# Attention and two mixtures on one Trainium2 core: decoding of 64-bit weights and the softmax start spread over the engines, with a new order

## The chip, the cores and the metric

The kernel runs on one core of one Trainium2 chip. The metric is the device time of one execution in microseconds (us). Five engines matter: TensorE (PE, with its weight loads shown as PEld), VectorE (DVE), ScalarE (ACT), GpSimd (POOL) and SyncE (SP), which issues nearly all DMAs.

## The reference

```
scores = scale * q @ k^T          # batch 2, 8 heads, 576 positions, 64 wide
                                  # heads 0-3: a local window of 32; heads 4-7: every 32nd position
attn   = exp(masked scores - row max);  attn /= sum(attn) + 1e-9
x      = attn @ v                 # as 1152 tokens x 512
h      = max(x @ w1, x @ w2, x @ w3)          # 512 -> 768, the first MLP
x2     = h @ w_out                            # 768 -> 512
out    = sum over 4 experts e of p[:, e] * (relu(x2 @ we1[e]) @ we2[e])    # 512 -> 1024 -> 512
```

w1, w2, w3 and w_out come as float64. [...] q, k, v, the expert weights and the output are float32.

## The kernel before

**Stages.** The tokens are cut into four blocks i: batch i // 2, and positions 0 to 255 (even i) or 256 to 575 (odd i), so 256 or 320 tokens each. For each block there are four head pairs p (0 and 1 local, 2 and 3 strided). Attention for (i, p) is made of four atoms: `aa` (scores in PSUM on PE, row maximum on DVE, negated and scaled by 0.125 into `anm`, exponentials on ACT with a sum per row), `an` (reciprocal of the sum on DVE, scaling on POOL), `at` (transposes on PE, copied out of PSUM to `pt` by ACT) and `ap` (product with v on PE, then a split of x in two float16 parts by ACT and DVE). The tiny operation that makes `anm` (L270, L272) runs on POOL for odd i and on DVE for even i (`ANM`).

**Weights.** Every matmul of the MLPs uses three float16 products (high x high, high x low, low x high), so each weight is scaled by a power of two and split in a high and a low float16 part. The first MLP's weights come in six groups `fc` (128 columns of w1, w2 and w3: 128 partitions x 1536 numbers, 1536 KB as 64-bit words), w_out in two groups of the same size. Four atoms prepare a group: `lw` (the load; there are two staging buffers, and one is free again when its group is decoded), `wa` (the largest value, which gives the scale), `wd` (the decoding) and `wp` (the split: ACT writes high, DVE writes low, L136 and L137). `lo`, `oa`, `od`, `os` and `op` do the same for w_out.

**Decoding** (`decode64`, L155 to L168) takes four passes over the 1536 numbers, which lie 8 bytes apart: ACT makes the top bits of the low word (L162); ACT takes 2^-112 off the exponent of the high word, in place (L163); DVE picks the sign out of the high word and joins it to the low word (L166, a `scalar_tensor_tensor` with two inputs); DVE shifts the high word by three bits and joins both (L167). If `wa` comes ahead of `wd`, the largest value is a DVE reduction over the raw words (L132); if it comes behind, it is bounded by an ACT sum of absolute values (L129). The decoded group lies in `r`, of which there is one buffer.

**First MLP and experts.** Atom `g` (block, fc) is the first MLP's hidden layer, with ACT, DVE and POOL making the maximum and the split; `go` is the product with w_out. The experts follow, with a form of the matrix product that takes seven block products (L564 to L566), and a second product (mm3, L350 to L352). The preparation of expert 0 (`ew`, `fw`, `xw`, `yw`) and the start of its first product (`m`) are atoms too.

**Order.** `ORDER` lists the atoms; each is traced in that order, and a planner at compile time, with its own costs, orders each engine's instructions from it. An engine runs its instructions in that fixed order, and SP issues its DMAs so as well.

## Time and profile before

| | us |
|---|---|
| three timed runs | 574.89, 577.31, 580.47 (median 577.31) |
| profiled execution: its span, first to last instruction (no other time of it is given) | 576.2 |
| busy in the span: PE, DVE, ACT, POOL | 555.6, 363.6, 265.1, 136.2 |
| mean granted TensorE clock over the span | 0.973 |

A busy time is the union of the engine's instructions; waiting is not in it. A busy PE can still be slow, because the granted clock (1.00 is 2.4 GHz, 0.50 is 1.2 GHz) is another column. A window row gives, for a stretch of the span, each engine's busy time with the count of its instructions, the granted clock and the share of the 16 DMA engines in use.

### The profile page before, as it was taken

Reading aid. Unit: us, or ns where it says so; the run is one execution under the profiler, and the core shown is the slowest. Engines: PE = TensorE matmul, PEld = TensorE weight load, DVE = VectorE, ACT = ScalarE, POOL = GpSimd, SP = SyncE. Lnnn points to the kernel's source line nnn. Section 1 sums busy time; section 2 is a strip of 40 time slices with the busy share of each in tenths; the row PEclk is TensorE's granted clock in tenths of the full one; section 3 lists DMA queues with packets and bytes.
Section 4 is the critical chain, followed back from the end, with each engine's and each line's share of the span. In section 5 each row is a group of like instructions: output and inputs, shape, how many; then the busy total and the mean of one; then the engine's idle time right before and its main releaser. Section 6 shows DMA issues by size and latency. Waiting matters only on the chain.

```text
span 576.2 us, 9839 instructions
## 1 busy us (share of the span) xinstructions
PE 555.6 (96%) x3968; PEld 380.2 (66%) x3968; DVE 363.6 (63%) x674; ACT 265.1 (46%) x561; POOL 136.2 (24%) x118
## 2 busy tenths in 40 slices
PE   6889899999999999899999999999999999999997
PEld 3778788878777778674447875446875446875444
DVE  3887799882781137988755775993765843765111
ACT  4778778681762123657726443605433610433000
POOL 1223374520121101322505211260221200221000
PEclk9588799999999999999999999999999999999999
DMA  8999338100040003004160000350000000000111
GB/s 292 334 359 292 103 136 294 50 2 2 1 147 1 1 1 114 34 1 148 73 219 0 1 2 1 109 178 6 2 1 1 1 0 1 2 1 0 56 55 56
DMA packets 16253, 44.33 MB, mean 77 GB/s; under 512 B 2296, under 2 KB 2552, under 8 KB 15440
## 3 DMA queue, kind: packets, MB, share of 16 engines
q1 hardware_dynamic: 16064, 43.41, 22.6%
q8 instruction: 31, 0.51, 0.4%
q10 hardware_dynamic: 144, 0.30, 0.2%
...
## 4 chain that ended last, share of the span: by engine, by line
PE 82%; DVE 5%; DMA 5%; ACT 4%; issue 2%; POOL 1%; SPq 1%; DVEq 0%; ACTq 0%; POOLq 0%
PE e L352 11%; PE e L350 11%; PE e L351 11%; PE w L564 9%; PE w L566 9%; PE w L565 9%; PE g L350 6%; PE g L351 6%; PE g L352 6%; DMA v<-in_vs_dram 3%; DMA v<-in_vl_dram 2%; PE sps L264 1%; PE tps L310 1%; ACT p L275 1%; PE ops L337 1%
## 5 line engine op out<-in xcount | busy, mean ns | idle before, releaser
L564 PE MATMUL w<-xops,w1ops 128*128 128x256 f16 (+1 forms) x448 | 127.9, 286 | 1.0 <-DVE c L572 1.0
L565 PE MATMUL w<-xops,w1ops 128*128 128x256 f16 (+1 forms) x448 | 128.0, 286 | 0.8 <-DVE xops L473 0.8
L566 PE MATMUL w<-xops,w1ops 128*128 128x256 f16 (+1 forms) x448 | 128.0, 286 | 0.0
L352 PE MATMUL g<-x,w 128*128 128x256 f16 (+1 forms) x288 | 82.4, 289 | 0.8 <-DVE w L137 0.8
L351 PE MATMUL g<-x,w 128*128 128x256 f16 (+1 forms) x288 | 83.1, 290 | 0.0
L350 PE MATMUL g<-x,w 128*128 128x256 f16 (+1 forms) x288 | 81.3, 289 | 1.5 <-DVE t L398 0.6
L586 POOL TENSOR_TENSOR h<-c,h 128x640 f16<-128x640 f32 (+1 forms) x30 | 40.0, 1335 | 173.9 <-ACT h L585 160.5
L699 DVE SCALAR_TENSOR_TENSOR x2acc<-e,coef,x2acc 128x512 f32<-128x512 f32 (+1 forms) x28 | 20.2, 727 | 69.5 <-PE e L352 69.5
L588 ACT ACTIVATE h<-c 128x512 f16<-128x512 f32 (+1 forms) x34 | 23.1, 680 | 86.3 <-DVE c L578 85.7
L350 PE MATMUL e<-st,h 128*128 128x512 f16 (+1 forms) x152 | 55.9, 368 | 0.0
L352 PE MATMUL e<-st,h 128*128 128x512 f16 (+1 forms) x152 | 55.9, 368 | 0.0
L351 PE MATMUL e<-st,h 128*128 128x512 f16 (+1 forms) x152 | 55.9, 368 | 0.0
L352 PE MATMUL e<-w,h 128*128 128x512 f16 x144 | 54.6, 379 | 0.0
L351 PE MATMUL e<-w,h 128*128 128x512 f16 x144 | 54.4, 379 | 0.0
L350 PE MATMUL e<-w,h 128*128 128x512 f16 x144 | 54.0, 379 | 0.0
L565 PEld LDWEIGHTS <-w1ops 128*128 128x128 f16 x448 | 43.8, 98 | 13.2 <-issue 1.4
L566 PEld LDWEIGHTS <-w1ops 128*128 128x128 f16 x448 | 43.8, 98 | 12.4 <-issue 1.4
L564 PEld LDWEIGHTS <-w1ops 128*128 128x128 f16 x448 | 43.8, 98 | 12.0 <-DVE c L577 0.2
L352 PEld LDWEIGHTS <-h 128*128 128x128 f16 x296 | 29.0, 98 | 33.2
L350 PEld LDWEIGHTS <-h 128*128 128x128 f16 x296 | 29.0, 98 | 32.3
L351 PEld LDWEIGHTS <-h 128*128 128x128 f16 x296 | 29.0, 98 | 32.0
L400 POOL TENSOR_TENSOR h<-t,h 128x256 f16<-128x256 f32 (+1 forms) x24 | 22.7, 950 | 85.5 <-ACT h L399 85.5
...
## 6 DMA issues: line engine op xcount, KB each, us to landing
...
qk<-in_qk1l_dram SPq DMA_DIRECT2D x4, 496.0 KB, 11.7
...
```

The lines of the kernel that those rows point to most:

```text
L264: nc.tensor.matmul(s3[:, j, :], qv[:, g, :], t[:, kstep * g : kstep * g + nk], start=False, stop=j == n - 1)
L275: nc.scalar.activation(p3[:, g, :], s3[:, j, :], AF.Exp, bias=ngm[:rows, g : g + 1], scale=0.125, accum_out=sm[:rows, g : g + 1],)
L350: nc.tensor.matmul(psum, lh, rh, start=i == 0, stop=False)
L351: nc.tensor.matmul(psum, lh, rl, start=False, stop=False)
L352: nc.tensor.matmul(psum, ll, rh, start=False, stop=i == n - 1)
L400: nc.gpsimd.tensor_tensor(hh[:, 1, fc, :], t1[:, :n], hh[:, 0, fc, :], ALU.subtract)
L564: nc.tensor.matmul(pt, wh, xh, start=k == 0, stop=False)
L565: nc.tensor.matmul(pt, wh, xl, start=False, stop=False)
L566: nc.tensor.matmul(pt, wl, xh, start=False, stop=k == 1)
L586: nc.gpsimd.tensor_tensor(lo, c[:, b], hi, ALU.subtract)
L588: nc.scalar.activation(hi, c[:, b], AF.Relu)
L699: nc.vector.scalar_tensor_tensor(a, pt[:, z], coef[:, t : t + 1], a, ALU.mult, ALU.add)
```

## The change

- **Decoding.** The sign is no longer joined by a two-input pass: a one-source pass over 16-bit halves writes the sign into the upper half of the low word (`SGN`: DVE for groups 0 to 3 and 7; for 4 to 6 POOL, which multiplies the high word by zero into a bfloat16). The pass for the low bits runs on DVE, POOL or ACT (`LOW`), and so does the exponent's (`REB`). The last joining pass stays on DVE.
- **Scales.** In the new order `wd` stands ahead of `wa` for groups 0, 1, 2 and 4 and both halves of w_out (before: for group 2), so five DVE reductions become ACT sums.
- **Split.** For groups 0 and 3 (`WLO` q) POOL scales in place, ACT copies to high, POOL subtracts to low. The others stay as they were.
- **Softmax start.** The row maximum comes out negated. `SUB` says for each (i, p) how the exponential gets it: `o`, as before, with the factor 0.125 on DVE always; `d`, DVE adds it to the scores, out of PSUM into SBUF, and ACT works from there; `p`, PE adds it in PSUM by a float32 matmul with the identity. `ACC` b (block 3, p 0) takes the row sums by a DVE reduction.
- **Copies of transposes** go to DVE for seven of sixteen (i, p) (`PTC`), and `ARS` swaps which blocks add 1e-9 on POOL.
- **Order.** A new `ORDER`. The load of weight group 0 is now the first on SP, ahead of all q and k, and groups 0 to 2 are decoded earlier relative to the attention.

```diff
-ANM = 'dpdp'
-ARS = 'pppd'
+SUB = 'ddooodpopooooodo'
+ACC = 'ggggggggggggbggg'
+SGN = 'ddddpppd'
+PTC = 'aaddaddaaaaaddda'
+LOW = 'dpdaaadd'
+REB = 'papppaad'
+WLO = 'qddqdd'
+ARS = 'dpdp'
...
 ORDER = """
-    lq02 lq00 lv01 lq01 lw0 lq03 aa00 lv00 lq20 vs0 aa01 aa02 wa0 wd0 an00 at00 an01 lw1 lv21 ap00 at01 lv20
-    an02 aa03 ap01 wp0 at02 an03 ap02 at03 aa20 ap03 lw2 vs2 wa1 an20 at20 lq22 lq21 aa21 wd1 aa22 lq23 an22
...
+    lw0 lq02 lq01 lq00 wd0 aa01 lv01 lq03 lq20 aa02 an02 wa0 aa00 aa03 lv00 vs0 lw1 an00 aa20 wd1 lv21 lq22 an03
+    lq23 aa23 at00 lv20 at02 vs2 an20 aa22 lw2 at20 an01 ap00 at01 lq21 at03 wd2 an22 aa21 wp0 wa1 lq12 an21 lw3
+    ap02 aa12 lq10 at21 lv10 lv11 an23 ap01 ap03 at22 lq13 lq11 ap21 aa11 wa2 an12 wp1 wa3 an11 aa10 lw4 vs1
+    lv31 ap22 an10 at23 at10 lq30 lq31 ap20 wd3 wd4 at12 ap23 aa13 an13 g00 g01 lw5 aa30 lo0 wp2 lq32 g20 wp3
...
+WHI = 'daadaa'
...
-        top = st64[g % 2].bitcast(U16).rearrange("p (n t) -> p n t", t=4)[:, :, 1]
-        nc.scalar.activation(lw, top, AF.Copy, bias=2.0**-14 - 0.5, scale=2.0**-13)
-        nc.scalar.activation(hw, hw, AF.Copy, scale=REBIAS)
+        half = st64[g % 2].bitcast(U16).rearrange("p (n t) -> p n t", t=4)
+        if LOW[g] == "a":
+            nc.scalar.activation(half[:, :, 0], half[:, :, 1], AF.Copy, bias=2.0**-14 - 0.5, scale=2.0**-13)
+        elif LOW[g] == "p":
+            nc.gpsimd.tensor_scalar(half[:, :, 0], half[:, :, 1], 2.0**-13, 2.0**-14 - 0.5, ALU.mult, ALU.add)
+        else:
+            nc.vector.tensor_scalar(half[:, :, 0], half[:, :, 1], 13, None, ALU.logical_shift_right)
+        if SGN[g] == "d":
+            nc.vector.tensor_scalar(half[:, :, 1], half[:, :, 3], 0x8000, None, ALU.bitwise_and)
+        else:
+            nc.gpsimd.tensor_scalar(half[:, :, 1].bitcast(BF16), hw, 0.0, 1.0, ALU.mult, ALU.mult)
+        if REB[g] == "a":
+            nc.scalar.activation(hw, hw, AF.Copy, scale=REBIAS)
+        elif REB[g] == "p":
+            nc.gpsimd.tensor_scalar(hw, hw, REBIAS, 1.0, ALU.mult, ALU.mult)
+        else:
+            nc.vector.tensor_scalar(hw, hw, REBIAS, None, ALU.mult)
         r = rp.tile([128, NP], F32, tag="r", name=nm("r")) if g < NF1 else hw
         gi, ri = hw.bitcast(I32), r.bitcast(I32)
-        nc.vector.scalar_tensor_tensor(lw, gi, -0x80000000, lw, ALU.bitwise_and, ALU.bitwise_or)
         nc.vector.scalar_tensor_tensor(ri, gi, 3, lw, ALU.logical_shift_left, ALU.bitwise_or)
...
-        ngm = sc.tile([128, 6], F32, tag="anm", name=nm("anm"))
         sm = sc.tile([128, 6], F32, tag="asm", name=nm("asm"))
         for g0 in range(0, ng, sb):
             n = min(sb, ng - g0)
...
                 st = ps.tile([128, 512], F32, tag="mm", name=nm("sps"))
             else:
                 st = psa.tile([128, 512], F32, tag="s", name=nm("sps"))
-            s3 = st[:rows, : n * nk].rearrange("p (g k) -> p g k", g=n)
+            flat = st[:rows, : n * nk]
+            s3 = flat.rearrange("p (g k) -> p g k", g=n)
             if loc:
                 mrhs = mkl[:, 0:4, :] if hf == 0 else mkl[:, 1:6, :]
             else:
                 mrhs = mks0[:, :n, :] if hf == 0 else mks1[:, :n, :]
-            nc.tensor.matmul(
-                st[:rows, : n * nk], identb[:, :rows], mrhs.rearrange("p g k -> p (g k)"), start=True, stop=False
-            )
+            nc.tensor.matmul(flat, identb[:, :rows], mrhs.rearrange("p g k -> p (g k)"), start=True, stop=False)
             for j in range(n):
                 g = g0 + j
                 nc.tensor.matmul(
                     s3[:, j, :], qv[:, g, :], t[:, kstep * g : kstep * g + nk], start=False, stop=j == n - 1
                 )
             gs = slice(g0, g0 + n)
-            nc.vector.tensor_reduce(mx[:rows, gs], s3, AX.X, ALU.max)
-            if ANM[i] == "p":
-                nc.gpsimd.tensor_scalar(ngm[:rows, gs], mx[:rows, gs], -0.125, 1.0, ALU.mult, ALU.mult)
+            nc.vector.tensor_reduce(mx[:rows, gs], s3, AX.X, ALU.max, negate=True)
+            top = mx[:rows, gs].unsqueeze(2).to_broadcast([rows, n, nk])
+            pf = p3[:, gs, :]
+            if SUB[4 * i + p] == "o":
+                nc.vector.tensor_scalar(mx[:rows, gs], mx[:rows, gs], 0.125, None, ALU.mult)
+                for j in range(n):
+                    g = slice(g0 + j, g0 + j + 1)
+                    acc_to = dict(accum_out=sm[:rows, g]) if ACC[4 * i + p] == "g" else {}
+                    nc.scalar.activation(pf[:, j], s3[:, j], AF.Exp, bias=mx[:rows, g], scale=0.125, **acc_to)
+                continue
+            if SUB[4 * i + p] == "p":
+                nc.tensor.matmul(s3, ident[:rows, :rows], top, start=False, stop=True, skip_group_check=True)
+                ef = s3
             else:
-                nc.vector.tensor_scalar_mul(ngm[:rows, gs], mx[:rows, gs], -0.125)
-            for j in range(n):
-                g = g0 + j
-                nc.scalar.activation(
-                    p3[:, g, :],
-                    s3[:, j, :],
-                    AF.Exp,
-                    bias=ngm[:rows, g : g + 1],
-                    scale=0.125,
-                    accum_out=sm[:rows, g : g + 1],
-                )
+                nc.vector.tensor_tensor(pf, s3, top, ALU.add)
+                ef = pf
+            if ACC[4 * i + p] == "b":
+                nc.scalar.activation(pf, ef, AF.Exp, scale=0.125)
+            else:
+                for j in range(n):
+                    nc.scalar.activation(
+                        pf[:, j], ef[:, j], AF.Exp, scale=0.125, accum_out=sm[:rows, g0 + j : g0 + j + 1]
+                    )
+        if ACC[4 * i + p] == "b":
+            nc.vector.tensor_reduce(sm[:rows, :ng], p3, AX.X, ALU.add)
...
-            nc.scalar.copy(ptt[:nk, : n * rows], tps[:nk, : n * rows])
+            if PTC[4 * i + p] == "a":
+                nc.scalar.copy(ptt[:nk, : n * rows], tps[:nk, : n * rows])
+            else:
+                nc.vector.tensor_copy(ptt[:nk, : n * rows], tps[:nk, : n * rows])
             pts_of[i, p].append((c0, n, ptt))
 
     def att_p(i, p):
...
 
     def split_w(fc):
         hi, lo = [ws[fc][j].rearrange("p w k f -> p (w k f)") for j in range(2)]
-        split(hi, lo, groups[fc][2], wsc[fc])
+        r = groups[fc][2]
+        if WLO[fc] == "d":
+            if WHI[fc] == "a":
+                nc.scalar.activation(hi, r, AF.Copy, scale=wsc[fc])
+            else:
+                (nc.gpsimd if WHI[fc] == "p" else nc.vector).tensor_scalar(hi, r, wsc[fc], 1.0, ALU.mult, ALU.mult)
+            nc.vector.scalar_tensor_tensor(lo, r, wsc[fc], hi, ALU.mult, ALU.subtract)
+        else:
+            nc.gpsimd.tensor_scalar(r, r, wsc[fc], 1.0, ALU.mult, ALU.mult)
+            nc.scalar.copy(hi, r)
+            nc.gpsimd.tensor_tensor(lo, r, hi, ALU.subtract)
```

## Rows read from the trace of the kernel before

**Rows 1.** Windows: stretch, width, busy by engine, clock, DMA share, GB/s.
```profile
10.00:30.00 20.00, 14.78 (x83) 11.78 (x84) 17.00 (x34) 16.21 (x50) 5.55 (x10) 0.56 1.02 336
30.00:70.00 40.00, 35.06 (x331) 30.09 (x329) 31.55 (x61) 31.79 (x96) 15.07 (x22) 0.84 0.85 260
70.00:130.00 60.00, 57.99 (x624) 49.83 (x621) 54.17 (x95) 45.31 (x118) 27.24 (x25) 1.00 0.33 116
130.00:260.00 130.00, 127.69 (x995) 96.88 (x994) 73.39 (x154) 55.61 (x105) 21.71 (x19) 1.00 0.10 33
```

**Rows 2.** Windows of 10 us inside the stretch 30 to 70, same columns.
```profile
40.00:50.00 10.00, 8.07 (x78) 6.68 (x78) 9.30 (x13) 9.15 (x30) 4.40 (x7) 0.83 1.02 319
...
60.00:70.00 10.00, 9.84 (x77) 8.68 (x78) 7.05 (x14) 8.15 (x21) 3.41 (x6) 0.66 0.33 89
```

**Rows 3.** Timeline, 37.5 to 42: start, us, instruction, [idle before <-releaser].
```profile
37.58 1.65 ACT L162 ACTIVATE st<-st 128x1536 int32<-128x1536 uint16 x1
...
41.93 0.36 PE L259 MATMUL sps<-mk,identb 128*128 128x480 bf16 x1 [1.98 <-ACT p L275]
```

**Rows 4.** Timeline, 55 to 60.5, same columns.
```profile
55.04 1.75 DVE L132 TENSOR_REDUCE vm<-v 108x1 f32<-108x1536 f32 x1 [1.83 <-DMA v<-in_vs_dram]
...
57.17 1.75 DVE L166 SCALAR_TENSOR_TENSOR st<-st 128x1536 int32<-128x1536 int32 x1
...
57.34 1.63 POOL L270 TENSOR_SCALAR anm<-amx 120x3 f32<-120x3 f32 x1 [2.00 <-DVE amx L268]
...
60.16 0.43 PE L259 MATMUL sps<-mk,identb 128*120 128x324 bf16 x1 [2.89 <-ACT p L275]
```

**Rows 5.** DVE groups by form, 0 to 180: busy us, mean ns, idle.
```profile
L166 DVE SCALAR_TENSOR_TENSOR st<-st 128x1536 int32<-128x1536 int32 x8 | 15.6, 1953 | 2.2 <-ACT st L163 2.2
L137 DVE SCALAR_TENSOR_TENSOR w<-r,s,w 128x1536 f16<-128x1536 f32 x6 | 11.1, 1843 | 0.3 <-ACT w L136 0.3
...
L132 DVE TENSOR_REDUCE mx<-st 128x1 bf16<-128x1536 f32 x5 | 8.7, 1743 | 0.5 <-DMA st<-in_w_dram 0.4
...
L397 DVE TENSOR_TENSOR t<-t,g 128x320 f32<-128x320 f32 x7 | 3.4, 481 | 7.1 <-PE g L352 5.6 <-ACT t L396 1.5
...
L105 DVE RECIPROCAL s<-sinv 128x1 f32<-128x1 f32 x6 | 0.9, 147 | 0.0
...
L182 DVE CAST identb<-ident 128x128 bf16<-128x128 f32 x1 | 0.2, 226 | 0.2 <-POOL ident masks.py:199 0.2
```

**Rows 6.** ACT groups by form, 0 to 180, same columns.
```profile
L162 ACT ACTIVATE st<-st 128x1536 int32<-128x1536 uint16 x8 | 13.2, 1651 | 1.8 <-DMA st<-in_wo_dram 1.7
...
L312 ACT COPY pt<-tps 108x360 f32<-108x360 f32 x8 | 3.7, 466 | 4.2 <-PE ops L337 4.2
...
L129 ACT ACTIVATE w<-r 128x1536 f16<-128x1536 f32 x1 | 1.5, 1484 | 0.3 <-DVE r L167 0.3
```

**Rows 7.** POOL groups by form, whole span, same columns.
```profile
L523 POOL TENSOR_TENSOR st<-st,st 128x1024 f32<-128x1024 f32 x3 | 7.9, 2640 | 29.9 <-DMA st<-in_we_dram 26.7 <-issue 3.2
L270 POOL TENSOR_SCALAR anm<-amx 120x3 f32<-120x3 f32 x8 | 8.8, 1102 | 9.6 <-DVE amx L268 9.5
...
L298 POOL TENSOR_TENSOR p<-p,ar 128x480 f32<-128x480 f32 x4 | 4.0, 991 | 4.2 <-DVE ar L297 4.2
```

**Rows 8.** PE group by form, 0 to 180, same columns.
```profile
L264 PE MATMUL sps<-qk 128*120 128x108 f32 x48 | 7.0, 283 | 0.0
```

**Rows 9.** Timeline at 87 us: a DVE instruction beside a long POOL one.
```profile
86.28 2.22 POOL L298 TENSOR_TENSOR p<-p,ar 128x480 f32<-128x480 f32 x2 [2.48 <-DVE ar L297]
...
87.32 2.79 DVE L166 SCALAR_TENSOR_TENSOR st<-st 128x1536 int32<-128x1536 int32 x1 [0.85 <-ACT st L163]
```

**Rows 10.** Timeline of the start: first DVE, PE and ACT work of the attention.
```profile
5.90 1.00 PE L264 MATMUL sps<-qk 128*128 128x64 f32 x8
...
8.08 1.21 DVE L132 TENSOR_REDUCE vm<-v 64x1 f32<-64x1024 f32 x1 [6.52 <-DMA v<-in_vs_dram]
...
10.06 0.34 ACT L275 ACTIVATE p<-sps,anm 128x96 f32<-128x96 f32 x1 [7.40 <-DVE anm L272]
```

More of the change, by code (lines that the diff above doesn't have):

```diff
@@ L37 @@
 ORDER = """
-    lq02 lq00 lv01 lq01 lw0 lq03 aa00 lv00 lq20 vs0 aa01 aa02 wa0 wd0 an00 at00 an01 lw1 lv21 ap00 at01 lv20
-    an02 aa03 ap01 wp0 at02 an03 ap02 at03 aa20 ap03 lw2 vs2 wa1 an20 at20 lq22 lq21 aa21 wd1 aa22 lq23 an22
-    lq10 ap20 aa23 an21 at21 ap21 wp1 at22 g00 lv11 an23 g01 lq12 lw3 lv10 wa3 at23 ap22 lq11 lv30 wd2 ap23
-    wa2 lq32 wd3 wp2 g20 g21 wp3 g03 aa11 an11 aa10 an10 aa12 vs1 lq13 lq30 at10 g23 at11 ap11 an12 lv31 lw4
-    ap10 at12 g02 wa4 wd4 wp4 lw5 lq31 wa5 lq33 wd5 aa13 aa30 wp5 an30 ap12 an13 aa33 g04 at13 ap13 aa31 vs3
-    at30 g24 ap30 lo0 an31 an33 aa32 g22 at31 at33 lo1 ap31 ap33 an32 at32 g25 oa0 od0 ap32 oa1 od1 os fo op4
-    op0 ew op1 g05 ew g10 fw ew op5 ew op2 op3 fw ew go20 go00 g11 ew ew go03 ew go23 go22 go21 ew go01 go02
-    ew xw g14 g12 g30 ew ew xw g32 ew g13 ew xw g15 ew ew g31 xw xw xw g33 g34 g35 ew xw cl fw xw xw go30 go10
-    go32 go13 go12 go31 m go33 fw m go11 m yw m fw yw yw yw fw yw yw fw fw yw yw yw
+    lw0 lq02 lq01 lq00 wd0 aa01 lv01 lq03 lq20 aa02 an02 wa0 aa00 aa03 lv00 vs0 lw1 an00 aa20 wd1 lv21 lq22 an03
+    lq23 aa23 at00 lv20 at02 vs2 an20 aa22 lw2 at20 an01 ap00 at01 lq21 at03 wd2 an22 aa21 wp0 wa1 lq12 an21 lw3
+    ap02 aa12 lq10 at21 lv10 lv11 an23 ap01 ap03 at22 lq13 lq11 ap21 aa11 wa2 an12 wp1 wa3 an11 aa10 lw4 vs1
+    lv31 ap22 an10 at23 at10 lq30 lq31 ap20 wd3 wd4 at12 ap23 aa13 an13 g00 g01 lw5 aa30 lo0 wp2 lq32 g20 wp3
+    g21 g03 ap10 lv30 at11 aa31 wa5 ap12 ap11 wd5 at13 vs3 g23 lq33 aa32 an30 g22 wa4 lo1 od1 g02 an32 at30 ap13
+    aa33 wp4 g10 ap30 oa1 wp5 od0 oa0 g04 g25 at32 an33 g14 ap32 os at33 an31 at31 ap31 ap33 g05 g24 fo ew op0
+    op1 ew fw op4 op2 ew op5 op3 go00 go20 ew go23 go21 go22 ew fw go02 g30 g12 fw go01 ew go03 g31 ew xw xw g33
+    ew ew g34 g11 ew fw ew g15 xw g32 xw ew xw g13 ew xw xw go10 g35 ew go30 ew go12 go33 cl go32 fw ew xw ew
+    go31 m m go11 go13 m yw fw yw fw yw xw fw yw yw yw yw m yw yw
 """
+WHI = 'daadaa'
 TINY = 2.0**-100
```

## The prediction

> **What bounds the kernel.** I read the windows first. PE works at the full clock and almost without a break from 130 us on, so time is to be had only where PE is idle or slow. I count a stretch's loss as idle time plus busy time x (1 - clock) [rows 1]. From 10 to 30 it is 5.2 + 14.8 x 0.44 = 11.7 us; from 30 to 70, 4.9 + 35.1 x 0.16 = 10.5; from 70 to 130, 2.0; from 130 to 260, 2.3. Together 26.5 us. In the same stretches DVE and ACT are busy for about 80% of the time up to 70, and DVE for 90% from 70 to 130. The DMA engines are full from 10 to 30 (share 1.02), and 0.85 from 30 to 70.
>
> Second, the timeline at PE's two long breaks between 30 and 70. PE stands 1.98 us before 41.93, for exponentials that ACT reaches only behind the two decoding passes of weight group 2, of which the first begins at 37.58 [rows 3]. It stands 2.89 us before 60.16: DVE's reduction of v comes first (55.04, 1.75 us), then POOL's tiny `anm` takes 1.63 us, because DVE's sign pass (57.17, 1.75 us) began just ahead of it and POOL ends only when that one does [rows 4]. After each break the clock falls: 0.83 in 40 to 50 and 0.66 in 60 to 70, against 1.00 in dense stretches [rows 1, 2]. So the first break costs 1.9 idle + 8.07 x 0.17 = 3.3 us, the second 2.9 + 9.84 x 0.34 = 6.2 us: 9.5 of the 10.5.
>
> **The change, engine by engine.** These sums are work in the stretch up to 130 us, not path.
>
> *DVE loses* eight sign passes of 1.953, five reductions of 1.743 and two low splits of 1.843 [rows 5]: 15.6 + 8.7 + 3.7 = 28.0 us. *It gains* ten one-source passes over 1536 numbers (five signs, four low, one exponent). No row shows one. The CAST, one source from SBUF to SBUF, takes 226 ns for 128, and a one-column operation 147 ns, so 0.62 ns a number: 1.10 us at the fast end; the reduction over the same 1536 takes 1.74 at the slow end [rows 5]. I take 1.10, as the CAST is nearest in kind: 11.0 us (17.4 at the other end). Twelve copies of transposes of 365 numbers on average, priced by the read of PSUM with 320 in 481 ns: 0.53 each, 6.3 us. Five subtractions `d`, of 379: 0.54 each, 2.7. One sum `b`, 0.65. Four more `anm` and four more 1e-9, at 0.15: 1.2. Sum 21.9, net **-6.1 us** (up to +0.3).
>
> The page "VectorE: DVE Perf Modes" of the Trainium skill (Mode 2×_2P) states that a one-source operation with both ends in SBUF passes two elements a cycle; by it the ten passes would be an estimated 9.5 us, and DVE's net -7.6. No row here has such a pass of this length.
>
> *ACT loses* five low passes and five exponent passes (same shape, both counted at 1.651) and twelve copies of 0.466, and gains five sums of 1.484 [rows 6]: -16.5 - 5.6 + 7.4 = **-14.7 us**. The split of groups 0 and 3 leaves ACT one pass, as before. Where `d` is used, ACT's exponential has the same count and reads SBUF: counted as nothing; it hides among the others.
>
> *POOL loses* the twelve `anm` (1.10 each, nearly all of it waiting) and gains ten one-source passes and two subtractions of 1536. Its own row of 480 in 991 ns gives 3.2 us for 1536; ACT's 1.65 for this shape is the fast end; I take 3.2, as it is POOL's own. The subtraction: 2.640 for 1024, so 4.0 [rows 7]. So +32 + 7.9 - 13.2 = **+27 us** (fast end, with 3.2 for the subtraction: +9.7). POOL has room: 15.1 of 40 us busy from 30 to 70 and 27.2 of 60 behind it [rows 1].
>
> **What of it lies on the path.**
>
> *Start (10 to 30).* The load of group 0, 1536 KB, goes ahead of all q and k on SP's queue; at 336 GB/s [rows 1] the first scores come 4.7 us later than at 5.90. But DVE was held by a reduction of v until 9.3, and ACT's first exponential came at 10.06 [rows 10]. Scores at 10.6, 1.0 of matmuls, a maximum and a subtraction of 0.5 each: about 12.2, some 2 us late. Against that, group 0 is decoded while the engines wait, and its passes no longer come between exponentials: 1 back. I take **+1.0**, bounds +4.7 (all of the delay) and -3 (its decoding, two ACT passes of 1.65, all won). The queue behind holds the same first eight transfers, so nothing later than 16 us is moved by this.
>
> *`p` matmuls.* Three of 344 columns in float32, 7.0 us / 48 for 108 columns [rows 8]: 0.47 each, 1.4, half in idle time: **+0.7** (0 to 1.4).
>
> *30 to 70.* Group 2's low and exponent passes leave ACT (DVE and POOL take them), and no `anm` is left on POOL, so both causes of the two breaks go, and with them the falls of the clock. What is late next: DVE's reduction of v still stands ahead of a maximum, and DVE has a subtraction more. I leave 1.0 for it: **-8.5**, bounds 0 and -10.5.
>
> *70 to 130.* Here too `anm` waits behind DVE passes, but PE has other work: half of 2.0, **-1.0** (0 to -2.0). *130 to 260.* The order of the experts' preparation changes; I see no sign for it: **0** (-2.3 to +2.3).
>
> Sum +1.0 + 0.7 - 8.5 - 1.0 = -7.8 us on the profiled execution's span of 576.2: 568.4. The page gives no other time of that execution; its span is 1.1 below the median of the runs, 577.31, which I add: **569.5 us**.
>
> **The rivals.**
>
> *A, no change.* The stretch's pace is the DMA's (share 1.02 from 10 to 30 [rows 1]) and the bytes are the same; a break that is taken out comes back at the next transfer, like the 1.83 us for which DVE waits for v at 55.04 [rows 4]. Against it: neither break of PE was a wait for a transfer that the change leaves as it is, save that one. Then only start, `p` and the 1.0 behind 70 count: 576.2 + 0.7 + 1.1 = 578. The one-source passes running at the slow end, so that the sign's new form saves little (DVE net +0.3), ends here too.
>
> *B, slower: POOL and DVE hold each other.* Rows 4 show POOL waiting for a two-input DVE pass, and a DVE pass that takes 1.75 alone takes 2.79 behind POOL's long multiplications [rows 4, 9]. Twelve long POOL passes, 40 us, meet a DVE busy 80 to 90%. If DVE waits for half of them, it loses 20 and keeps 6.1 of relief: +13.9, half of which PE feels: +7; with start and `p`, 576.2 + 8.7 + 1.1 = **586**. It decides once DVE waits for more than about 6 us in all. For it: DVE is the fuller engine. Against it: in rows 4 it is POOL that waits, and that costs only the decoding's own delay.
>
> The page "SBUF — State Buffer" of the Trainium skill (Who interferes with whom) has the rule: one pair of ports, held for a whole instruction, by POOL or by a DVE instruction with two SBUF inputs, and also by a one-source one in a two-port mode. By that last part the ten new DVE passes would hold POOL as well, which no row here shows.
>
> *C, a larger gain.* With ACT 14.7 us lighter and group 0 ready early, PE is dense from 30 on and 4 us of the start's loss go too: -10.5 - 2.0 - 2.3 - 4 + 0.7 = -18: 559.
>
> **The numbers.** A difference of 1% (5.8 us) is about what this kernel's runs can tell from none: faster is under 571.5, slower above 583.1. Forecast 0.48, spread over 563 to 576 by its bounds, two thirds of it under 571.5 (0.33). C 0.20. A 0.15. B 0.17. Faster 0.33 + 0.20 = 0.53; same 0.15 + 0.15 = 0.30; slower 0.17. The range reaches from C's centre to the near edge of B: 558 to 582, leaving out most of B and the far half of C's lower side, some 0.2.
>
> **What would show it.** Right: no break of PE over 1.5 us between 30 and 70, a clock above 0.95 there, ACT's busy time down by 10 to 15 us up to 130, and one-source DVE passes near 1.1 us. Start right: first exponential at 11 to 12.5 us. Wrong: DVE passes of 3 us and more beside long POOL ones (B); breaks as long as before with transfers as their releasers (A); a loss behind 130 of over 4 us, which no term here holds.

## The result and the profile after

The change is slower by 0.9%: 581.25 us against 576.32 us, medians of 12 runs each, ratio 1.0092 [1.0066, 1.0117]. The forecast was 569.5. The profiled execution took 581.21 us with a span of 579.1, so some 2 us lie outside a span (1.8 in later executions of the kernel before). By that the profiled execution of before (span 576.2) was some 1.7 us over its median: the spans differ by 2.9 us, the medians by 4.9.

Windows of the changed kernel, same columns as [rows 1]:

```profile
10.00:30.00 20.00, 17.20 (x82) 14.34 (x82) 16.63 (x37) 9.58 (x45) 10.70 (x7) 1.00 1.03 326
30.00:70.00 40.00, 34.12 (x323) 28.19 (x323) 36.33 (x69) 28.96 (x86) 14.95 (x16) 0.96 0.68 240
70.00:130.00 60.00, 57.86 (x581) 48.70 (x581) 47.30 (x92) 38.03 (x93) 34.83 (x28) 1.00 0.37 126
130.00:260.00 130.00, 128.41 (x1043) 98.63 (x1042) 80.34 (x161) 60.83 (x126) 22.87 (x20) 1.00 0.10 34
```

From 10 to 130, ACT is 16.7 us lighter than before, DVE only 2.5, POOL 12.6 heavier. But the changed kernel has also done less by then: 986 matmul records from 10 to 130 against 1038, and in 30 to 70 323 against 331. So the price of the change is better read over the whole span, from the page of the changed kernel:

```profile
PE 559.4 (97%) x3977; PEld 381.9 (66%) x3977; DVE 370.8 (64%) x695; ACT 256.6 (44%) x544; POOL 150.6 (26%) x114
```

Against before that is DVE +7.2 us, ACT -8.5 and POOL +14.4.

The groups by form up to 130 us (busy us, mean ns), in the order DVE, ACT, POOL, answer to [rows 5, 6, 7]:

```profile
L176 DVE TENSOR_SCALAR st<-st 128x1536 uint16<-128x1536 uint16 x5 | 12.1, 2419 | 1.0 <-ACT st L170 0.9
L187 DVE SCALAR_TENSOR_TENSOR r<-st 128x1536 int32<-128x1536 int32 x6 | 11.3, 1886 | 1.7 <-POOL st L182 1.7
L174 DVE TENSOR_SCALAR st<-st 128x1536 uint16<-128x1536 uint16 x4 | 7.9, 1975 | 7.7 <-DMA st<-in_w_dram 6.4 <-DMA st<-in_wo_dram 1.3
...
L184 DVE TENSOR_SCALAR st<-st 128x1536 f32<-128x1536 f32 x1 | 0.9, 947 | 0.0
...
L170 ACT ACTIVATE st<-st 128x1536 uint16<-128x1536 uint16 x3 | 11.1, 3688 | 0.0
...
L178 POOL TENSOR_SCALAR st<-st 128x1536 bf16<-128x1536 f32 x3 | 11.8, 3945 | 5.4 <-ACT st L170 3.5 <-DVE st L174 1.9
L182 POOL TENSOR_SCALAR st<-st 128x1536 f32<-128x1536 f32 x4 | 6.4, 1595 | 17.3 <-DVE st L176 10.5 <-DVE ars L323 6.6
L419 POOL TENSOR_TENSOR w<-r,w 128x1536 f16<-128x1536 f32 x2 | 6.2, 3106 | 0.0
L172 POOL TENSOR_SCALAR st<-st 128x1536 uint16<-128x1536 uint16 x1 | 3.6, 3620 | 0.1
```

A 64-bit weight is loaded as two 32-bit words, from which the passes rebuild a float32 number. Every pass that stores a 16-bit half of such a word is dear on its engine: 1.98 and 2.42 us on DVE (1.87 where nothing holds it), where 1.10 was forecast and the one pass with a 32-bit store (L184) took 0.95; 3.69 on ACT, where the same function with a 32-bit store took 1.65 [rows 6]; 3.62 to 3.95 on POOL, whose 32-bit pass (L182) takes 1.60.

Two waits of PE from the timeline. First POOL's subtraction, the DVE pass that starts 0.27 us behind it, and PE:

```profile
27.97 3.10 POOL L419 TENSOR_TENSOR w<-r,w 128x1536 f16<-128x1536 f32 x1
...
28.24 4.54 DVE L176 TENSOR_SCALAR st<-st 128x1536 uint16<-128x1536 uint16 x1
...
33.09 0.37 PE L368 MATMUL ops<-pt,v 64*64 64x64 f32 x2 [1.48 <-DVE x L376]
```

The pass takes 1.87 alone, so POOL held it for 2.7 us, and the small DVE operation that PE needs stands behind it. That is rival B's mechanism, with a one-source pass.

Second, ACT's 16-bit pass, the exponentials and the copy for `g` behind it, and PE:

```profile
52.97 3.64 ACT L170 ACTIVATE st<-st 128x1536 uint16<-128x1536 uint16 x1
56.36 0.34 ACT L306 ACTIVATE p<-p 128x96 f32<-128x96 f32 x1
...
57.69 0.35 ACT L437 COPY t<-g 128x256 f32<-128x256 f32 x1
...
58.09 0.27 PE L381 MATMUL g<-x,w 128*128 128x256 f16 x1 [1.51 <-ACT t L437]
```

This is the break of [rows 3] over again, in another place: a decoding pass on ACT ahead of small work that PE waits for.

The start, timeline of PE, DVE and ACT, answers to [rows 10]:

```profile
7.94 1.87 DVE L174 TENSOR_SCALAR st<-st 128x1536 uint16<-128x1536 uint16 x1 [6.37 <-DMA st<-in_w_dram]
...
8.12 1.23 PE L279 MATMUL sps<-mk,identb 128*128 128x384 bf16 x4 [2.49 <-DMA mk<-in_masks_dram]
...
9.84 1.87 DVE L176 TENSOR_SCALAR st<-st 128x1536 uint16<-128x1536 uint16 x1
...
16.20 0.87 DVE L286 TENSOR_REDUCE amx<-sps 128x4 f32<-128x384 f32 x2
...
17.57 0.28 ACT L306 ACTIVATE p<-p 128x96 f32<-128x96 f32 x1 [0.80 <-DVE p L300]
...
22.04 1.65 PE L297 MATMUL sps<-amx,ident 128*128 128x384 f32 x2 [1.44 <-DVE amx L286]
...
26.11 1.80 PE L282 MATMUL sps<-qk 128*128 128x64 f32 x8
...
43.45 0.81 PE L297 MATMUL sps<-amx,ident 120*120 120x324 f32 x2 [1.16 <-DVE amx L286]
```

DVE decodes group 0 first, and ACT's first exponential comes at 17.57 (10.06 before). The clock column shows 1.00 from 10 to 30, but eight score records at 26.11 (a float32 matmul leaves two, so these are four matmuls) take 1.80 us where the same took 1.00 in [rows 10]. This is the lower level, and the record of its fall is missing: the trace holds no clock record before 37.5 us. p_nosub below, with the same work of the other engines, records 0.50 there.

To compare PE over stretches without that column I price each matmul by what its shape takes back to back at the full clock, and call the rest of the time lost. Cumulative us, with the held-order kernels of the next section (named p_):

| | lost by 10 | by 30 | by 70 | by 130 | by 330 | PE work | span |
|---|---|---|---|---|---|---|---|
| before | 4.7 | 17.8 | 29.8 | 33.3 | 36.7 | 535.3 | 576.2 |
| changed | 6.8 | 18.6 | 30.2 | 34.4 | 37.2 | 538.1 | 579.1 |
| p_low32 | 6.7 | 17.9 | 24.8 | 28.9 | 31.1 | 538.1 | 572.9 |
| p_low32_nosign | 6.9 | 17.1 | 22.3 | 25.0 | 27.8 | 538.1 | 569.7 |
| p_warm18 | 4.6 | 16.2 | 28.3 | 32.5 | 35.3 | 539.8 | 579.0 |
| p_nosub | 6.3 | 19.5 | 32.3 | 36.6 | 40.6 | 535.8 | 580.2 |
| p_lwlate | 4.7 | 20.8 | 35.6 | 40.9 | 44.7 | 538.1 | 586.6 |

Differences of less than about half a microsecond in this table hang on how a shape is priced. Over the span the changed kernel loses as much as before (41.0 and 40.9 us), and it has 2.8 us more of PE work.

### The profile page after: what moved, and what is told of

It is laid out like the page before. It is cut to its first block, busy times and chain, and to the rows that moved or that the text cites. A ratio compares the mean times of both kernels' runs of the same rounds, so it can differ in the third digit from the quotient of the medians.

```text
span 579.1 us, 9843 instructions
## 1 busy us (share of the span) xinstructions
PE 559.4 (97%) x3977; PEld 381.9 (66%) x3977; DVE 370.8 (64%) x695; ACT 256.6 (44%) x544; POOL 150.6 (26%) x114
## 4 chain that ended last, share of the span: by engine, by line
PE 81%; DVE 9%; DMA 4%; ACT 3%; issue 2%; POOL 0%; DVEq 0%; SPq 0%
PE e L381 11%; PE e L383 11%; PE e L382 11%; PE w L605 9%; PE w L607 9%; PE w L606 9%; PE g L381 6%; PE g L383 6%; PE g L382 6%; DMA st<-in_wo_dram 3%; DVE st L176 2%; DMA st<-in_w_dram 1%; DVE vm L139 1%; PE ops L368 1%; DVE st L174 1%
## 5 line engine op out<-in xcount | busy, mean ns | idle before, releaser
L605 PEld LDWEIGHTS <-w1ops 128*128 128x128 f16 x448 | 43.8, 98 | 11.9
L383 PEld LDWEIGHTS <-h 128*128 128x128 f16 x296 | 28.9, 98 | 33.2
L381 PEld LDWEIGHTS <-h 128*128 128x128 f16 x296 | 28.9, 98 | 32.4
L382 PEld LDWEIGHTS <-h 128*128 128x128 f16 x296 | 28.9, 98 | 32.0
L441 POOL TENSOR_TENSOR h<-t,h 128x256 f16<-128x256 f32 (+1 forms) x24 | 24.3, 1017 | 85.5 <-ACT h L440 85.4
```

Source lines behind the costliest of these rows:

```text
L381: nc.tensor.matmul(psum, lh, rh, start=i == 0, stop=False)
L382: nc.tensor.matmul(psum, lh, rl, start=False, stop=False)
L383: nc.tensor.matmul(psum, ll, rh, start=False, stop=i == n - 1)
L441: nc.gpsimd.tensor_tensor(hh[:, 1, fc, :], t1[:, :n], hh[:, 0, fc, :], ALU.subtract)
L605: nc.tensor.matmul(pt, wh, xh, start=k == 0, stop=False)
```

## The experiments

The theories that the expectations name. S: the first weight load, put ahead of masks and scores, costs the start. H: the 16-bit stores are dear. P: PE's new work lies on the path. L: POOL's long passes hold DVE. K: the lower clock behind PE's early break costs the time. O or F: the order that the planner makes from `ORDER`, fitted to the parts and their durations, is what matters, so that a part alone or a small edit loses by being planned anew.

Ratios are to the kernel before on the same chip, with 95% intervals, five rounds each. A point is 1% of the time. The difference of two ratios is good to about 0.3 points between a held kernel (below) and the changed one, and to 0.4 or 0.5 elsewhere. The first twelve let the planner order the engines anew; the last six do not.

**The parts by themselves** (before with the named functions or constants of the changed kernel).

`b_order`, the order alone:

```diff
 ORDER = """
-    lq02 lq00 lv01 lq01 lw0 lq03 aa00 lv00 lq20 vs0 aa01 aa02 wa0 wd0 ...
+    lw0 lq02 lq01 lq00 wd0 aa01 lv01 lq03 lq20 aa02 an02 wa0 aa00 aa03 ...
```

> The kernel before with the new order alone (old decoding, softmax, copies and split). Theory S (the load of weight group 0 ahead of q, k and the masks starts the attention late and leaves PE at its lower clock to about 37 us) expects most of the loss here: +3 to +5 us against before, and a break of PE of about 2.5 us before 8 us. Theory H (the 16-bit stores of the decoding are dear) and theory P (new PE work: the float32 matmuls of the softmax start and of the scales) expect 0 to +1. The prediction on record expected +1 from this part.

`b_decode`, the new `decode64` and `split_w` in the old order:

```diff
-        nc.vector.scalar_tensor_tensor(lw, gi, -0x80000000, lw, ALU.bitwise_and, ALU.bitwise_or)
+        if SGN[g] == "d":
+            nc.vector.tensor_scalar(half[:, :, 1], half[:, :, 3], 0x8000, None, ALU.bitwise_and)
+        else:
+            nc.gpsimd.tensor_scalar(half[:, :, 1].bitcast(BF16), hw, 0.0, 1.0, ALU.mult, ALU.mult)
```

> The kernel before with the new decoding and the new split of groups 0 and 3, in the old order, softmax and copies as before. H expects 16-bit passes of 1.9 us on DVE, 3.6 on ACT and POOL and +2 to +5 us; S and P expect about 0; the prediction's sums (DVE and ACT relieved) expect -2 to -4.

`b_softmax`, the new `att_a`, `att_t` and `ARS` in the old order:

```diff
-ANM = 'dpdp'
-ARS = 'pppd'
+SUB = 'ddooodpopooooodo'
+ACC = 'ggggggggggggbggg'
+PTC = 'aaddaddaaaaaddda'
+ARS = 'dpdp'
```

> The kernel before with the new softmax start, the copies of transposes shared with DVE and the 1e-9 operations swapped, in the old order with the old decoding. The prediction's step for 30 to 70 us expects -4 to -8: no anm on POOL, so the break before 60 us goes. P expects +1 to +3 (three float32 matmul chunks of 0.5 to 0.8 us each on PE, nothing won).

`b_order_decode` and `b_order_softmax` join two of these edits each.

> The kernel before with the new order, the new decoding and the new split; old softmax start, copies and 1e-9 operations. Theory F (the order fits the places and durations of all the parts together, so a part alone loses) has two forms: if order and decoding are the pair that belongs together, the +20 and +22 us of each alone fall to +3 or less here; if the softmax belongs in the fit as well, +8 or more remains. Adding the measured parts up (no fit at all) would give +42.

> The kernel before with the new order and the new softmax start, copies and 1e-9 operations; old decoding and split. If order and decoding are the pair, this stays near order alone plus softmax, +18 to +26. If order and softmax are the pair, +3 to +8.

| order | decoding | softmax | ratio |
|---|---|---|---|
| new | old | old | 1.0346 [1.0314, 1.0377] |
| old | new | old | 1.0375 [1.0343, 1.0407] |
| old | old | new | 1.0112 [1.0083, 1.0141] |
| new | new | old | 1.0338 [1.0293, 1.0383] |
| new | old | new | 1.0167 [1.0131, 1.0202] |
| new | new | new | 1.0092 [1.0066, 1.0117] |

The parts don't add. Order and decoding cost about 3.5% each alone and together; with the other two in place the decoding is worth -0.75 points (1.0167 to 1.0092) and the softmax -2.5. New decoding and softmax in the old order were not run together. No single part came out as expected: the order alone cost 20 us (S had 3 to 5), the decoding 22 (H had 2 to 5), the softmax start 6 (the prediction's step had -4 to -8, P 1 to 3). b_order_decode kept 19 us, as F had it if the softmax belongs in the fit; b_order_softmax, 10 us, lies between F's two ranges. Since the planner ordered each of these kernels anew, the ratios are no prices of the parts.

**Two edits of the kernel before.** `b_sign`, the 16-bit one-source sign on DVE for all eight groups, nothing else:

```diff
+        nc.vector.tensor_scalar(half[:, :, 1], half[:, :, 3], 0x8000, None, ALU.bitwise_and)
...
-        nc.vector.scalar_tensor_tensor(lw, gi, -0x80000000, lw, ALU.bitwise_and, ALU.bitwise_or)
```

> The kernel before with the one-source 16-bit sign pass on DVE for all eight groups and nothing else of the change (low and exponent passes on ACT in 32 bits, old split, order, softmax). Theory H (16-bit stores): the pass takes 1.9 us in place of 1.95 for the two-input one, so nothing is won: 0 to +2 us. The prediction's price (1.1 us a pass) expects -1 to -3. A rival, F (the order is fitted to the durations and places of the instructions, and any change of parts alone loses): +5 us or more even here.

Measured 1.0001 [0.9977, 1.0026]. The group by form:

```profile
L164 DVE TENSOR_SCALAR st<-st 128x1536 uint16<-128x1536 uint16 x8 | 15.7, 1966 | 0.2 <-ACT st L162 0.2
```

15.7 us for eight passes, where the old form had 15.6 [rows 5]: the new form of the sign saves nothing, as H had it. F, in the form that any part alone loses 5 us or more, is wrong here: the order was planned anew, and it cost nothing.

`b_lw0first`, before with the first weight load ahead of all others:

```diff
-    lq02 lq00 lv01 lq01 lw0 lq03 ...
+    lw0 lq02 lq00 lv01 lq01 lq03 ...
```

> The kernel before with the load of weight group 0 ahead of q and k in its order, nothing else. Theory S (the start) expects +2 to +4 us with a break of PE of 2.5 us before 8 us. The run with that load put back in the changed kernel lost 10 us, which S does not explain; if an early decoded group 0 is a gain by itself, 0 to -3 here; F expects a loss of +5 or more by disordering alone.

Measured 1.0140 [1.0104, 1.0176], some 8 us, more than S had and within F's "5 or more". The order was planned anew, so what the early load costs by itself is not shown.

**The decoding without POOL.** `b_decode_nopool`, b_decode with every pass kept off POOL:

```diff
-SGN = 'ddddpppd'
-LOW = 'dpdaaadd'
-REB = 'papppaad'
-WLO = 'qddqdd'
-WHI = 'daadaa'
+SGN = 'dddddddd'
+LOW = 'dadaaadd'
+REB = 'aaaaaaad'
+WLO = 'dddddd'
+WHI = 'aaaaaa'
```

> The kernel before with the new decoding, but nothing of it on POOL: signs all on DVE, the low pass of group 1 and the exponent passes of groups 0, 2, 3 and 4 on ACT, the old split; old order. Theory L (POOL's long passes, 1.6 to 3.9 us, hold DVE and stand ahead of POOL's own multiplications of the attention) expects most of the 20 us of b_decode gone: +3 to +6 against before. H alone expects them to stay in good part (+10 or more, with the low passes on ACT at 3.7 us). F expects +10 or more too, without 16-bit passes being on the path.

Measured 1.0160 [1.0121, 1.0200], against 1.0375: 9 us, between L's range (3 to 6) and that of H and F (10 or more). Groups by form up to 180 us, of b_decode:

```profile
L402 DVE SCALAR_TENSOR_TENSOR w<-r,s,w 128x1536 f16<-128x1536 f32 x4 | 11.2, 2797 | 4.0 <-ACT w L399 4.0
...
L290 DVE TENSOR_SCALAR anm<-amx 128x4 f32<-128x4 f32 x8 | 5.8, 728 | 0.0
```

The same forms took 1.84 (low split, [rows 5]) and 0.21 us (tiny operation) in the kernel before, and 2.17 and 0.19 in b_decode_nopool. So in this order POOL and DVE do hold each other, as B said, and POOL's share is about two points of the 3.75, as far as two runs with an order each can tell. In the changed kernel the low split is back at 1.81 and 28.24 is the one long hold. The rest are short: up to 130 us DVE's instructions ran 12 us in all over the shortest of their form, and 6 in the kernel before. The longest of these are tiny operations, 1.26 us at 41.15 and 1.25 at 87.61, behind POOL's decoding passes.

**Small edits of the changed kernel.** `a_lw0fifth`, `a_no_pe_sub`, `a_low32`, `a_warm18`, in this order:

```diff
-    lw0 lq02 lq01 lq00 wd0 aa01 lv01 lq03 ...
+    lq02 lq01 lq00 lv01 lw0 wd0 aa01 lq03 ...
```

> The changed kernel with the load of weight group 0 put back behind the first three q and k loads and the first v load; all else as changed. S expects -3 to -4 against the changed kernel (to 577, no break of PE before 8 us, first exponentials 3 to 4 us earlier); H and P expect no difference (581).

```diff
-SUB = 'ddooodpopooooodo'
+SUB = 'ddooodoooooooodo'
```

> The changed kernel without the float32 matmuls that add the maximum on PE (the two places take the form o). Theory P (new PE work on the engine that is the bound) expects -2 to -3 us against the changed kernel, 578 to 579. Otherwise 0 or, by F, a loss.

```diff
-            nc.scalar.activation(half[:, :, 0], half[:, :, 1], AF.Copy, bias=2.0**-14 - 0.5, scale=2.0**-13)
+            nc.scalar.activation(lw, half[:, :, 1], AF.Copy, bias=2.0**-14 - 0.5, scale=2.0**-13)
-            nc.gpsimd.tensor_scalar(half[:, :, 0], half[:, :, 1], 2.0**-13, 2.0**-14 - 0.5, ALU.mult, ALU.add)
+            nc.gpsimd.tensor_scalar(lw, half[:, :, 1], 2.0**-13, 2.0**-14 - 0.5, ALU.mult, ALU.add)
-            nc.vector.tensor_scalar(half[:, :, 0], half[:, :, 1], 13, None, ALU.logical_shift_right)
+            nc.vector.tensor_scalar(lw, lw, 29, None, ALU.logical_shift_right)
```

> The changed kernel with the low pass stored in 32 bits on all engines (ACT and POOL write the int32 word, DVE shifts the int32 word by 29); the sign pass behind it still stores 16 bits. H expects the passes at 1.65 (ACT), 1.6 (POOL) and 0.95 (DVE) in place of 3.69, 3.62 and 1.98, some 12 us less work, and -1 to -4 us against the changed kernel. F expects no gain or a loss, since the order was not made for it.

```diff
-NWARM = 10
+NWARM = 18
```

> The changed kernel with 18 idle matmuls at the start in place of 10 (0.43 us each, their result is not used), so that PE is busy until the first scores' data land near 8 to 9 us. Theory K (what the early break costs is the lower clock behind it, under which PE works until about 37 us) expects the first attention matmuls at the full clock (eight of 96 columns in 1.0 us, not 1.9) and -1 to -4 us against the changed kernel. If the clock falls again by itself because the early attention is thin, no difference: 0 to +1.

Measured 1.0278 [1.0249, 1.0308], 1.0249 [1.0212, 1.0287], 1.0131 [1.0095, 1.0167], 1.0305 [1.0266, 1.0343]: every one of them is slower than the changed kernel's 1.0092, even with eight more warming matmuls in PE's idle start (the 32-bit low words by 0.4 points, which is at the edge of what two such ratios can tell). S, P, H and K had forecast gains here, or at most no difference; F had no gain or a loss. The traces show why these ratios can't be read as prices: of DVE's 695 instructions at most 611 stand in a common sequence in a_warm18 and the changed kernel. Each edit got another order.

**Held orders.** The next kernels take the same edits and fix each engine's order to the changed kernel's, by edges of issue order, without waits (`seq` is an engine's list; `p_lwlate` makes its edit in SP's list):

```diff
+        for x, y in zip(seq, seq[1:]):
+            tc.add_manual_dep(own[e][y], own[e][x].name, info, reason="pin")
```

> The changed kernel with the shift of the second words written as whole 32-bit words, and every engine held to the order of instructions that the changed kernel has (edges of issue order alone, no waits). The changed kernel is at 1.009 of the kernel before. Theory H (the 16-bit stores are dear): the ScalarE pass falls from 3.69 to near 1.65 us, the GpSimd one from 3.62 to near 1.6, the span by 3 us or more: ratio 1.004 or less. Theory F (the order in which the planner puts the work is what matters, and the passes lie beside other work): with the order held the direct effect is all that is left, 0 to 2 us: ratio 1.006 to 1.010. Either way an edit with a held order should not lose.

> The changed kernel with 18 warming matmuls instead of 10, every engine held to the order of the changed kernel. Without the held order the same edit measured 1.0305. Theory K (the PE break of 2.5 us before 8.12 us lowers the clock, which costs the span 2 to 6 us): the first score matmuls run near 1.0 us for eight of 96 columns instead of 1.86, and the ratio is 0.999 to 1.006. Theory F: the 21 points that the unheld edit lost were the planner's new order, so held it is within 0.004 of 1.009; if later PE breaks take back what the clock gives, exactly that. If the loss comes back with the order held (1.02 or more), F falls.

> The changed kernel with the first weight load issued fifth on its queue, behind three score loads and one value load, every other engine held to the order of the changed kernel. Without the held order the same edit measured 1.0278. Theory S (the weight load put first delays the masks and the first score loads): the mask lands near 5 us instead of 8.1, the first score matmul starts 2 to 3 us earlier, the clock does not fall at 10 us, ratio 0.999 to 1.006. Theory F with the decoding on the path at the start: the first weights land 1 to 2 us later and hold the decoding as much, no gain: 1.007 to 1.012. If 1.02 or more comes back with the order held, F falls.

In `p_nosub` besides:

```diff
-                nc.tensor.matmul(s3, ident[:rows, :rows], top, start=False, stop=True, skip_group_check=True)
```

> The changed kernel without the three float32 matmuls that subtract the row maxima of two attention tiles in PSUM (the exponentials of those two tiles are then not shifted), every engine held to the order of the changed kernel. Without the held order, with the same subtraction given to ScalarE's bias instead, it measured 1.0249. Theory P (the added PE work lies on the path): PE has 4 us less at the low clock and some 2.2 at the full one, and no wait of 2.6 us on the maxima; the span falls by 2 to 5 us: ratio 1.001 to 1.006. Theory F with PE waiting for others there anyway: within 0.003 of 1.009.

| edit | planned anew | held |
|---|---|---|
| 32-bit low words | 1.0131 [1.0095, 1.0167] | **1.0025 [1.0008, 1.0041]** |
| 18 warming matmuls | 1.0305 [1.0266, 1.0343] | 1.0112 [1.0095, 1.0129] |
| weight load fifth | 1.0278 [1.0249, 1.0308] | 1.0229 [1.0207, 1.0250] |
| no PE subtraction | 1.0249 (on ACT's bias) | 1.0147 [1.0126, 1.0169] (left out) |

The traces show the held order: in p_warm18, p_lwlate and p_nosub all 695 DVE instructions stand in the changed kernel's sequence. The changed kernel with its order held and no edit was not run; the span of p_warm18, 579.0 us against 579.1, gives no sign that holding by itself costs or wins anything.

*p_low32:* theory H holds, and F's range (1.006 to 1.010) is missed. The low words' store width costs the change 0.67 points, 3.9 us (give or take 1.7). Min, median and max ns of the low passes by line, in p_low32 (ACT, POOL, DVE), and the 16-bit sign pass left on DVE:

```profile
L170 ACT ACTIVATE st<-st x3: 1643/1667/1671, 48.5 to 73.8; 128x1536 int32<-128x1536 uint16 x3
...
L172 POOL TENSOR_SCALAR st<-st x1: 1569/1569/1569, 22.6 to 22.6; 128x1536 int32<-128x1536 uint16 x1
...
L174 DVE TENSOR_SCALAR st<-st x4: 954/964/1255, 7.7 to 106.9; 128x1536 int32<-128x1536 int32 x4
...
L176 DVE TENSOR_SCALAR st<-st x5: 1871/1884/1902, 8.7 to 107.9; 128x1536 uint16<-128x1536 uint16 x5
```

Same count, about half the time or less. On ACT and POOL only the store differs; DVE's 32-bit form also reads whole words. PE runs the same instructions in the same order in both kernels, so its two breaks can be followed, to 30.38 (33.09 in the changed kernel) and 52.05 (58.09):

```profile
30.38 0.68 PE L368 MATMUL ops<-pt,v 64*64 64x64 f32 x16 [1.71 <-DVE x L376]
...
52.05 0.28 PE L381 MATMUL g<-x,w 128*128 128x256 f16 x1
```

The break behind ACT's pass is gone. The one behind DVE's sign pass, which still stores 16 bits, stays, although the pass is not held here and takes 1.87 us. In p_low32_nosign (below), where it takes 0.24, the same matmul waits 0.18:

```profile
29.23 0.68 PE L368 MATMUL ops<-pt,v 64*64 64x64 f32 x16 [0.18 <-DVE x L376]
```

By the pricing of the table, most of p_low32's gain in 30 to 70 lies between 40 and 50. Windows of 10 us, changed kernel and then p_low32:

```profile
40.00:50.00 10.00, 8.14 (x72) 6.33 (x71) 9.11 (x20) 6.89 (x25) 3.54 (x4) 0.83 0.87 307
```

```profile
40.00:50.00 10.00, 10.00 (x114) 8.63 (x115) 8.73 (x17) 8.52 (x23) 3.03 (x4) 1.00 0.97 271
```

PE is idle for 1.9 us and falls to the lower level in the one, and does neither in the other. This is the gain that the prediction had described for this stretch.

*p_warm18:* PE loses 1.9 us less by 330 us (2.2 less by 10 us), but has 1.7 us more of work. PE's timeline:

```profile
11.51 1.13 PE L282 MATMUL sps<-qk 128*128 128x96 f32 x8 [0.45 <-DMA qk<-in_qk0l_dram]
...
16.93 0.77 PE L105 MATMUL rows<-ident,mx 128*128 128x128 f32 x2 [2.17 <-ACT w L136]
...
17.91 1.86 PE L282 MATMUL sps<-qk 128*128 128x96 f32 x8
```

The full rate is there at 11.51 and gone at 17.91, behind a wait of 2.17 us which is 0.84 in the changed kernel, where PE comes to it later. At 16.93 PE stands where it stands in the changed kernel (16.91): ACT's `w` sets the pace, and a faster PE only waits longer. Theory K, which had 0.999 to 1.006, falls: the early break is not what costs the time. What the lower level behind it costs is not shown, since it came back. And since the two kernels with 18 warming matmuls have the same instructions, the 1.9 points between them are the order's alone; for the low words it is 1.1 points.

*p_lwlate:* here the edit does cost 1.4 points with nothing else moved. DVE and PE, timeline:

```profile
12.73 1.87 DVE L174 TENSOR_SCALAR st<-st 128x1536 uint16<-128x1536 uint16 x1 [11.17 <-DMA st<-in_w_dram]
...
21.69 0.77 PE L105 MATMUL rows<-ident,mx 128*128 128x128 f32 x2 [5.95 <-ACT w L136]
```

The first weights land 4.8 us later (12.73 against 7.94), DVE's first maxima stand behind their decoding, and PE stands 5.95 us. So with this order the early load is needed: theory S in its plain form (0.999 to 1.006) falls too. By its expectation F falls as well, which had no loss of this size (1.02 or more) once the order was held. What the run shows is narrower: a held order can be the cause of a loss itself, as here DVE's order makes everything wait for the late weights. A load and the order behind it belong together.

*p_nosub:* 2.3 us less PE work, and no gain: 0.55 points slower by the ratios, 0.8 us by the medians. Theory P falls, and F's range (within 0.003 of 1.009) is missed too. The windows of 10 us, changed kernel and then p_nosub:

```profile
10.00:20.00 10.00, 9.16 (x41) 8.40 (x40) 8.32 (x12) 4.01 (x20) 1.55 (x1) 1.00 1.03 321
20.00:30.00 10.00, 8.04 (x42) 5.94 (x42) 8.30 (x26) 5.57 (x27) 9.15 (x6) 1.00 1.02 332
```

```profile
10.00:20.00 10.00, 8.63 (x37) 7.70 (x36) 8.32 (x12) 3.99 (x20) 1.56 (x1) 0.50 1.03 326
20.00:30.00 10.00, 6.41 (x40) 5.42 (x40) 8.30 (x27) 5.61 (x27) 9.12 (x6) 0.50 1.03 350
```

DVE, ACT and POOL do the same work in the same time; PE only waits longer. It has lost 0.9 us more by 30 and 2.1 more by 70, which is the removed work turned into waiting: the other engines set the pace there. The 1.3 us that it loses beyond that, behind 70, are not explained. Nor is the gap between 0.55 points (3.2 us) and 0.8 us: the two kernels were measured on different chips, each against its own runs of the kernel before (574.08 and 576.32 us).

**The sign's share.** Both start from p_low32. `p_low32_or` puts the old two-input sign back in DVE's five groups; `p_low32_nosign` cuts all eight sign passes to 64 columns, so that the other weights' signs are left out:

```diff
-            nc.vector.tensor_scalar(half[:, :, 1], half[:, :, 3], 0x8000, None, ALU.bitwise_and)
+            nc.vector.scalar_tensor_tensor(lw, hw.bitcast(I32), -0x80000000, lw, ALU.bitwise_and, ALU.bitwise_or)
```

> The kernel with 32-bit low words and the held order of the changed kernel (1.0025 by itself), and in the five groups whose sign VectorE makes, the sign put in by the old operation with two inputs on whole 32-bit words instead of the one-source 16-bit pass. Theory H (what a 16-bit store costs): the 16-bit pass took 1.88 us, the two-input one took 1.75 us undisturbed in the kernel before, so five of them give back under 1 us: ratio 0.999 to 1.003. If the one-source form was the better one beside GpSimd's passes (the prediction's ground for it), the passes grow by waits and the ratio is 1.004 or more.

```diff
+            nc.vector.tensor_scalar(half[:, :64, 1], half[:, :64, 3], 0x8000, None, ALU.bitwise_and)
+            nc.gpsimd.tensor_scalar(half[:, :64, 1].bitcast(BF16), hw[:, :64], 0.0, 1.0, ALU.mult, ALU.mult)
```

> The kernel with 32-bit low words and the held order, and every sign pass (five on VectorE, three on GpSimd) cut to 64 of its 1536 columns, so that the signs of the other weights are left out: what the change would be worth if the sign cost next to nothing. Theory H: some 9 us of VectorE and 11 us of GpSimd go, by the rate at which the low words' 14 us moved the span (4 us) that is 3 to 6 us: ratio 0.992 to 0.997, which is the gain that the prediction's prices stood for. Theory F (with this order the passes lie beside other work, PE is the bound): 0.999 to 1.004.

Measured 1.0023 [1.0004, 1.0043] and 0.9944 [0.9918, 0.9969]. The old form takes 1.75 us again:

```profile
L176 DVE SCALAR_TENSOR_TENSOR st<-st x5: 1748/1758/1760, 8.9 to 108.0; 128x1536 int32<-128x1536 int32 x5
```

So the form of the sign on DVE is worth nothing here either, and the sign at all (9.4 us of DVE and 11.5 of POOL, of which the cut passes keep 1.2 and 3.7) is worth 0.8 points, 4.7 us (give or take 1.8), within H's range and outside F's. The low words' passes had lost 11.9 us, where the expectation has 14. With low words at 32 bits and a sign for next to nothing the change would be a gain of 0.6%. No complete version beat the kernel before; p_low32 and p_low32_or come within 0.3% of it.

## Why the prediction was wrong

**The step that failed is "I take 1.10, as the CAST is nearest in kind".** The CAST stores contiguous 16-bit numbers; nine of the ten new DVE passes store 16-bit halves of words that lie 8 bytes apart. They took 1.88 alone, over the slow end (1.74) that the prediction kept for the range, and the price of ACT's low passes, kept at 1.65, was 3.69. The estimate was right for a 32-bit store, which one of the ten has: 0.95 in the changed kernel (L184), 0.96 for the low passes in p_low32. The page "VectorE: DVE Perf Modes" of the Trainium skill (Mode 2×_2P), two elements a cycle for one source in SBUF, agrees with that 0.96 but not with 1.88; the measurement decides.

With the order held, the low words' store costs 0.67 points (p_low32) and the sign 0.81 (p_low32_nosign). Together they turn a loss of 0.9% into a gain of 0.6%. That is not the whole miss, since the forecast was a gain of 1.4% and p_low32_nosign has nearly no sign, which is less than the prediction's own price for it. In that kernel PE loses 8.9 us less than before by 330, against the 8.5 that the prediction added up for its stretches: with the passes nearly free the mechanism gives what was forecast. The rest lies in PE's new work (2.8 us, not 0.7) and in the profiled execution of before, which was some 1.7 us over its median. 581.25 lies within the range of 558 to 582, but the time moved the other way.

By its own terms:

- *DVE -6.1, ACT -14.7, POOL +27.* Measured over the span: +7.2, -8.5, +14.4. ACT's miss is its three low passes at 3.69. POOL was over-priced (32-bit passes 1.60, not 3.2; subtraction 3.1, not 4.0), DVE under-priced.
- *Start +1.0.* Lost by 30 us: +0.8. The size was right by luck, the way was not: exponentials from 17.57, not 12.2, and the matmuls at the lower level, against group 0 being ready.
- *`p` matmuls +0.7.* Each of the three takes 0.81 us at 43.45 and 1.65 at 22.04, not 0.47. The price was a misreading: the 48 of [rows 8] are records, two for each float32 matmul, so a matmul of 108 columns takes 0.29 us and one of 344 some 0.93. All new PE work is 2.8 us. But p_nosub shows that taking the three out gives nothing back in the changed kernel; in p_low32_nosign this was not tried.
- *30 to 70, -8.5.* Measured 12.0 to 11.6, so -0.4. This is where the forecast gain went. That "both causes of the two breaks go" was true; new ones of the same kind took their place, 16-bit passes ahead of small work on ACT (1.51 at 58.09) and on DVE (1.48 at 33.09). In p_low32 the stretch loses 6.9 and in p_low32_nosign 5.2: -5.1 and -6.8. The gain hung on the passes' price.
- *70 to 130, -1.0; behind, 0.* Measured +0.7 and -0.6.
- *Span to median +1.1.* It is about 2, so the sum started from an execution some 1.7 us above the median.

Of the signs of being right, three came out nearly as named although the gain did not: the longest break between 30 and 70 is 1.51 us, the recorded clock there 0.96, and ACT is lighter by 16.7 us up to 130. But PE is idle for 5.9 us in that stretch all the same, in breaks of 1.51 us and less, the clock record is incomplete, and ACT was not the bound. The two other signs, the passes' price and the time of the first exponential, failed as the forecast did.

What no step held: that the planner's order and the durations belong together. The same instructions in two orders differ by 1.1 and 1.9 points (low words, warming matmuls), more than the whole change. Of the new order the prediction priced the early load (in the start's term) and the experts' preparation ("I see no sign for it: **0**"); the order alone, planned for the old parts, costs 3.5%.

Of the rivals, A had the mechanism in its last sentence: passes at the slow end, "so that the sign's new form saves little"; by b_sign it saves nothing at all. Its 578 leaves out most of the new PE work and the low words' store on ACT and POOL. B has some right: its sign, DVE passes of 3 us and more, came out once (4.54), and DVE's waits inside instructions, 12 us against 6 before, grew by about the 6 us at which B was to decide. But p_low32 has 11 us of them too, and a span 6.2 us shorter than the changed kernel, so the loss does not hang on them. By the page "SBUF — State Buffer" of the Trainium skill (Who interferes with whom) a one-source DVE pass in a two-port mode shares a lock with POOL; the 4.54 at 28.24 agrees. Whether a pass that takes 1.88 us is in such a mode no run shows.

What stays open: where p_nosub loses behind 70, and how much of the changed kernel's order is fitted to the dear passes. An order planned for the 32-bit passes exists in a_low32 (1.0131), and it is worse than the held one.
